# A batched attention and feed-forward kernel: part of q loaded first, four score pairs computed ahead, and bulk loads placed later in the queue

## Chip, cores and metric

One NeuronCore of one Trainium2 chip runs the whole kernel. The metric is the device time of one execution in microseconds (us). Three runs of the kernel before took 929.06, 928.07 and 927.72 us; their median is 928.07 us.

## What is computed

The reference is an attention with two mixings over heads, and a feed-forward layer on its result. Batch 4, 12 heads, 448 positions, head width 64, model width 768, hidden width 2048, all in 32-bit floats.

```python
scores = scale * np.matmul(q, k.transpose(0, 1, 3, 2))
scores = np.einsum('bhij,hg->bgij', scores, w_pre)
scores = scores - np.max(scores, axis=-1, keepdims=True)
attn = np.exp(scores)
attn = attn / (np.sum(attn, axis=-1, keepdims=True) + 1e-09)
attn = np.einsum('bhij,hg->bgij', attn, w_post)
attn_out = np.matmul(attn, v)
x = attn_out.transpose(0, 2, 1, 3).reshape(B * S, H * D)
h = x @ w_in
g = h * (1.0 / (1.0 + np.exp(-1.702 * h)))
return g @ w_out
```

## The kernel before

**Scores.** The queries of a batch are cut into four chunks: three of 120 rows and one of 88 (`chunk`, L204). The 12 heads make six pairs. `scores` (L216) multiplies a chunk of a pair's queries with its keys into two PSUM banks, `keep_scores` (L244) copies both banks to SBUF on ScalarE or VectorE, and `send_scores` (L248) writes the pair to a DRAM scratch `sd` of that chunk. The scratch is there to change the layout: `gather` (L256) reads ten query rows of all 12 heads back as one tile `r` of 120 partitions, which needs all six pairs of the chunk.

**Steps.** Ten query rows are one step: 12 steps to a chunk, 45 to a batch, 180 in all (the last of a batch is smaller). A step mixes heads with one product (`mix`, L266, tile `mx`), takes the row maximum on VectorE (`peak`), the exponential on ScalarE (`expo`), scales the second mixing's weights by the row sums on GpSimd (`shifted`, `weigh_mix`) and multiplies again (`post_whole`, L310, tile `pp`). There are four `r` buffers, so that four steps are gathered ahead. After the 12 steps of a chunk `context` (L383) multiplies with v in two halves (tile `av`, one PSUM bank), and ScalarE and VectorE bring the result into x as a pair of 16-bit parts.

**Weights and feed-forward.** The weights of the feed-forward layer come in 16 pieces (two kinds, eight slices). Each is loaded in three parts of 512 KB (L466), rounded and split on VectorE and ScalarE (tile `w_f`, some 18 VectorE instructions), and stored to DRAM as a 16-bit pair `wd` (L532); the sum of squares of a piece goes through TensorE (`pp<-w_m`, L108). From about step 53 on the feed-forward products of the first batch (`hidden`, tile `h`, L557; `project`, tile `po`, L595) fill TensorE beside the steps of the later batches. After the last step only feed-forward work is left.

**What sets the order.** The program is written out at build time. The head (L775 to L845) is in a fixed order: loads of k and q in thirds, ten products on ones, the six score pairs of the first chunk, each sent for its first 48 rows only (`FRONT`), four gathers, the remaining 72 rows of each pair, and 16 more products on ones (`idle_products`), whose results are not used. Behind it a list scheduler (`add`, `run_all`) holds a model of the engines and of the DMA queue, takes tasks by due step, and so fixes the order on each engine. On the chip every engine runs its own instructions strictly in that order and waits on semaphores. All DMAs are issued by SyncE (SP), one after the other; one issue waits until the eighth issue before it has landed. The scheduler's rule is in `run_all`: a DMA starts at the earliest when the eighth before it is over.

## Time and profile before

| | |
|---|---|
| median of 3 runs | 928.07 us |
| the profiled execution | 930.12 us |
| its span, first to last instruction | 928.4 us |
| PE busy | 897.2 us, 97% of the span |
| VectorE, ScalarE, GpSimd busy | 589.4, 593.3, 337.8 us |
| mean granted TensorE clock | 0.992 |
| moved by DMA | 196.76 MB, mean 212 GB/s |

PE is TensorE; its busy time is modelled for matmuls that overlap, so that a busy PE may still run slowly. A granted clock of 1.00 is the upper of its two levels, 2.4 GHz, and 0.50 the lower; a number between says how a stretch is shared by both. A matmul of 32-bit data has two records. The times of rows count from the first instruction of the span. A window's row gives, behind its length, how long each engine was busy in it.

### The profile page before, as it was taken

The numbers are of one execution on the slowest core, as the hardware profiler recorded it, in microseconds if no ns is written. First come the engines' busy times: TensorE is split into PE (matmuls) and PEld (weight loads), VectorE is DVE, ScalarE is ACT, GpSimd is POOL, SyncE is SP. The second block draws the span as 40 slices with busy tenths as digits, with TensorE's granted clock in tenths as the row PEclk, the third lists the DMA queues.
The fourth block names the chain that finished last, engine by engine and source line by source line (L and its number), as shares of the span: only waits on it lengthen the run. The fifth ranks groups of instructions, "written<-read, shape, count | busy, mean of one in ns | idle before, by whom it ended". The sixth has DMA issues, their size and how long they took to land.

```text
span 928.4 us, 18998 instructions
## 1 busy us (share of the span) xinstructions
PE 897.2 (97%) x6972; PEld 535.5 (58%) x6972; DVE 589.4 (63%) x1342; ACT 593.3 (64%) x1328; POOL 337.8 (36%) x532
## 2 busy tenths in 40 slices
PE   7879989999999999989999999999999999999998
PEld 5455656656566566655656555555656666545554
DVE  2678787687789978977567656567555554332233
ACT  2668787697875776765696776666675665324342
POOL 0212222221225313546346744455344553203431
PEclk9999999999999999999999999999999999999999
DMA  7878999997988796669576575567443422343322
GB/s 235 288 257 298 321 305 329 320 314 230 335 294 287 231 299 207 204 194 328 168 249 221 162 238 162 164 176 255 140 154 111 129 99 83 123 133 132 136 75 88
DMA packets 66256, 196.76 MB, mean 212 GB/s; under 512 B 7699, under 2 KB 32403, under 8 KB 66163
## 3 DMA queue, kind: packets, MB, share of 16 engines
q1 hardware_dynamic: 66162, 195.54, 65.1%
q8 instruction: 55, 0.90, 0.4%
q14 instruction: 39, 0.31, 0.1%
HBM read 138.89 MB, written 56.62 MB: 211 GB/s over the span
## 4 chain that ended last, share of the span: by engine, by line
PE 75%; DVE 9%; DMA 6%; ACT 5%; issue 2%; POOL 2%; SPq 1%; ACTq 0%; POOLq 0%; DVEq 0%
PE po L595 20%; PE h L557 20%; PE mx L271 12%; PE pp L316 5%; PE av L394 3%; PE av L405 3%; PE qk L225 3%; PE qk L235 3%; DMA r<-sd 2%; PE pp L353 2%; PE pp L355 2%; PE pp L354 2%; DVE nm L278 2%; ACT e L285 1%; ACT waste L96 1%
## 5 line engine op out<-in xcount | busy, mean ns | idle before, releaser
L557 PE MATMUL h<-x,wt 128*128 128x448 f16 x1152 | 246.8, 352 | 3.2 <-DMA wt<-wd 2.9
L595 PE MATMUL po<-g,wt 128*128 128x448 f16 x1152 | 239.7, 352 | 4.3 <-DVE th L576 2.4
L271 PE MATMUL mx<-r,wa 120*120 120x448 f32 x360 | 172.3, 563 | 5.2 <-DMA r<-sd 3.1
L557 PEld LDWEIGHTS <-wt 128*128 128x128 f16 x1152 | 109.2, 98 | 115.5 <-issue 26.4
L285 ACT ACTIVATE e<-mx,nm 120x448 f32<-120x448 f32 x180 | 113.9, 633 | 96.4 <-DVE nm L278 84.5
L595 PEld LDWEIGHTS <-wt 128*128 128x128 f16 x1152 | 109.9, 98 | 108.4 <-issue 16.7
L296 POOL TENSOR_SCALAR rs<-sm 120x1 f32<-120x1 f32 x180 | 46.8, 260 | 336.6 <-ACT e L285 333.3
L278 DVE TENSOR_REDUCE nm<-mx 120x1 f32<-120x448 f32 x180 | 111.4, 619 | 46.3 <-PE mx L271 44.9
L623 POOL TENSOR_TENSOR acc<-acc,pt 128x448 f32<-128x448 f32 x64 | 72.8, 1138 | 117.3 <-ACT pt L617 116.9
L316 PEld LDWEIGHTS pp<-wr,e 120*112 120x112 f32 x720 | 84.4, 177 | 40.9 <-issue 18.9
L576 DVE SCALAR_TENSOR_TENSOR th<-th,h 128x448 f32<-128x448 f32 x64 | 39.6, 619 | 105.9 <-ACT th L572 105.5
L340 POOL TENSOR_TENSOR a<-w,a 120x448 f16<-120x448 f32 (+1 forms) x90 | 95.8, 1064 | 26.3 <-POOL w L326 17.6
L316 PE MATMUL pp<-wr,e 120*112 120x120 f32 x720 | 91.4, 270 | 6.0 <-POOL wr L306 6.0
L246 ACT COPY sc<-qk 120x448 f32<-120x448 f32 (+1 forms) x150 | 74.5, 532 | 15.7 <-PE qk L225 11.3
L619 DVE SCALAR_TENSOR_TENSOR acc<-po,ct,acc 128x448 f32<-128x448 f32 x104 | 70.3, 679 | 22.0 <-PE po L595 21.1
L271 PEld LDWEIGHTS mx<-r,wa 120*120 120x120 f32 x360 | 57.8, 184 | 37.4 <-issue 16.2
L326 POOL TENSOR_SCALAR w<-e,rs 120x448 f32<-120x448 f32 (+1 forms) x90 | 60.5, 672 | 40.8 <-DVE rs L301 35.0
L617 ACT ACTIVATE pt<-po,ct 128x448 f32<-128x448 f32 x64 | 40.6, 634 | 51.1 <-PE po L595 51.0
L334 ACT ACTIVATE a<-e,rs 120x448 f16<-120x448 f32 (+1 forms) x90 | 60.3, 670 | 18.4 <-DVE rs L301 17.2
L380 DVE TENSOR_TENSOR p<-pp,p 112x480 f16<-112x480 f32 (+1 forms) x90 | 58.4, 649 | 19.2 <-ACT p L376 18.9
L306 POOL TENSOR_SCALAR wr<-wp,rs 120x120 f32<-120x120 f32 (+1 forms) x90 | 47.4, 527 | 54.0 <-DVE rs L301 33.7
L353 PE MATMUL pp<-wp,a 120*112 120x120 f16 x360 | 62.3, 217 | 0.0
(123 smaller groups left out, 1323.0 us busy)
## 6 DMA issues: line engine op xcount, KB each, us to landing
wt<-wd SPq DMA_DIRECT2D x64, 768.0 KB
r<-sd SPq DMA_DIRECT2D x176, 210.0 KB
sd<-sc SPq DMA_DIRECT2D x66, 420.0 KB
w<-in_moe_w_in_dram SPq DMA_DIRECT2D x24, 512.0 KB
w<-in_moe_w_out_dram SPq DMA_DIRECT2D x24, 512.0 KB
wd<-w_p SPq DMA_DIRECT2D x16, 768.0 KB
sd<-sc SPq DMA_DIRECT2D x24, 308.0 KB
out_dram<-acc SPq DMA_DIRECT2D x24, 224.0 KB
```

Of the source, the lines that this page charges most:

```text
L246: (nc.scalar.copy if eng == "A" else nc.vector.tensor_copy)(t[:n, x, :], two[x][:n, :S])
L271: nc.tensor.matmul(mx[:K, :S], st["wa", b][:K, :K], row.pop(("r", i))[:K, :], start=True, stop=True)
L278: nc.vector.tensor_reduce(nm[:K], row["mx", i][:K, :S], axis=AX.X, op=ALU.max, negate=True)
L285: nc.scalar.activation(e[:K], row.pop(("mx", i))[:K, :S], AF.Exp, bias=row.pop(("nm", i))[:K, 0:1], scale=1.0, accum_out=sm[:K, 0:1],)
L316: nc.tensor.matmul(pp[:CP, jc * K:(jc + 1) * K], e[:K, jc * CP:(jc + 1) * CP], wr[:K, :, :n], start=True, stop=True,)
L326: nc.gpsimd.tensor_scalar(w[:K], e[:K], row["rs", i][:K, 0:1], 1.0, op0=ALU.mult, op1=ALU.mult)
L340: nc.gpsimd.tensor_tensor(a2[:K], row.pop(("w", i))[:K], row["a1", i][:K], op=ALU.subtract)
L353: nc.tensor.matmul(o, a1[:K, js], wp1[:K, :, :n], start=True, stop=False)
L557: nc.tensor.matmul(h, w[:, i, c, fc * 128:(fc + 1) * 128], x[:, j, c, :], start=(n == 0), stop=(n == len(terms) - 1),)
L595: nc.tensor.matmul(po, w[:, j, fc, e * 128:(e + 1) * 128], g[:, i, fc, :], start=(n == 0), stop=(n == len(terms) - 1),)
L619: nc.vector.scalar_tensor_tensor(a, po, c, a, op0=ALU.mult, op1=ALU.add)
L623: nc.gpsimd.tensor_tensor(a, a, st.pop(("pt", u, e)), op=ALU.add)
```

## The change

Three things are changed. The first third-by-third loads of q bring only the first 240 of 448 columns (two chunks of queries); the other 208 columns come by three loads of their own, behind the back sends of the first chunk. Four of the six score pairs of the second chunk (`SOON`) are computed, copied and sent in the head, between the first chunk's pairs and the first step, and idle products fall from 16 to 4. And the scheduler gets a kind of load, "late" (the weight parts, their stores, v, and q and k of later batches): it holds such a DMA in its model until its queue has at most 1.5 us of work left. The due time of a score send falls from x + 2 to x.

```diff
--- before.py
+++ after.py
@@ -121,6 +121,17 @@
         t = st[name, b, i] = flow.tile(SH[name], F32, name=f"{name}{use}{i}_{b}", tag=tag, bufs=THIRDS)
         w = t.shape[1]
         nc.sync.dma_start(out=t, in_=SRC[name][b][:, i * w:(i + 1) * w])
+
+    def load_front(i, n):
+
+        t = st["q", 0, i] = flow.tile(SH["q"], F32, name=f"qf{i}_0", tag=f"qp{i}")
+        w = t.shape[1]
+        nc.sync.dma_start(out=t[:, :, :n], in_=q[0][:, i * w:(i + 1) * w, :n])
+
+    def load_back(i, n):
+        t = st["q", 0, i]
+        w = t.shape[1]
+        nc.sync.dma_start(out=t[:, :, n:], in_=q[0][:, i * w:(i + 1) * w, n:])
 
     def load_whole(name, b, i):
 
@@ -718,6 +729,8 @@
                     s = max(room, j["from"], free.get(e, 0.0))
                     if j["size"] and len(lanes) >= 8:
                         s = max(s, lanes[-8])
+                    if j["kind"] == "late":
+                        s = max(s, DMA["free"] - 1.5)
                     best.append((s + (j["bias"] if e != j["eng"][0] else 0.0), s, j))
                 if best:
                     t = min(x[0] for x in best) + LOOK
@@ -773,8 +786,8 @@
         return k
 
     for i in range(THIRDS):
-        for name in "kq":
-            load_whole(name, 0, i)
+        load_whole("k", 0, i)
+        load_front(i, 2 * CI)
     for i, w in enumerate((w_pre, w_post)):
         nc.sync.dma_start(out=wrep[:, i, :], in_=w.unsqueeze(0).to_broadcast([GI, H, H]))
     nc.sync.dma_start(out=wall, in_=w_post.unsqueeze(0).to_broadcast([128, H, H]))
@@ -823,12 +836,16 @@
     tags = [("gen", 3), ("mx", 2), ("pp", 2)]
     homes = [("sc", 3), ("g", 2), ("sc", 3), ("g", 2), ("sc", 3), ("acc", 1)]
     kept = []
-    FRONT = 48
+    FRONT, SOON = 48, 4
+
+    def head_pair(c, pr, tag, home):
+        two = scores(0, c, pr, tag)
+        kept.append(scores_home(0, c, pr, home))
+        for x in range(2):
+            keep_scores(0, c, x, kept[-1], two, "AD"[x])
+
     for pr in range(NPAIR):
-        two = scores(0, 0, pr, tags[pr % 3])
-        kept.append(scores_home(0, 0, pr, homes[pr]))
-        for x in range(2):
-            keep_scores(0, 0, x, kept[pr], two, "AD"[x])
+        head_pair(0, pr, tags[pr % 3], homes[pr])
         send_scores(0, 0, pr, kept[pr], 0, FRONT)
     nc.vector.tensor_tensor(
         w_mix,
@@ -837,16 +854,22 @@
         op=ALU.mult,
     )
     mixing(0)
+    for pr in range(SOON):
+        head_pair(1, pr, tags[pr % 3], (f"wt{pr % 2}", 2))
     mixing_pair()
     for i in range(AHEAD):
         gather(i)
     for pr in range(NPAIR):
         send_scores(0, 0, pr, kept[pr], FRONT)
-    idle_products(16)
-
-
-    free.update({"PE": 17.0, "A": 15.0, "D": 16.0, "G": 3.0, "SP": 21.0})
-    DMA["free"] = 22.0
+    for i in range(THIRDS):
+        load_back(i, 2 * CI)
+    for pr in range(SOON):
+        send_scores(0, 1, pr, kept[NPAIR + pr])
+    idle_products(4)
+
+
+    free.update({"PE": 17.5, "A": 16.0, "D": 18.0, "G": 3.0, "SP": 22.0})
+    DMA["free"] = 26.0
     lanes.extend([24.0] * 8)
     held["sc"] = [23.0, 23.5, 24.0]
     r_home = {i: [] for i in range(N)}
@@ -932,7 +955,7 @@
                     {"A": 0.53, "D": 0.62}, bias=0.3)
             banks[n].append(k)
             both.append(k)
-        s = add("SP", 0.4, lambda: send_scores(b, c, pr, t["t"]), both, x + 2, size=0.43)
+        s = add("SP", 0.4, lambda: send_scores(b, c, pr, t["t"]), both, x, size=0.43)
         sc += both + [s]
         sends.setdefault((b, c), []).append(s)
 
@@ -975,11 +998,11 @@
 
     def whole_load(name, b, i, x):
         h = in_home[name, b, i]
-        return add("SP", 0.4, lambda: load_whole(name, b, i), gated_by(x), x, size=0.459, takes=[(f"{name}p{i}", h)])
+        return add("SP", 0.4, lambda: load_whole(name, b, i), gated_by(x), x, size=0.459, takes=[(f"{name}p{i}", h)], kind="late")
 
     def staged_load(name, b, i, use, x):
         h = []
-        return add("SP", 0.4, lambda: load(name, b, i, use), gated_by(x), x, size=0.459, takes=[("op", h)]), h
+        return add("SP", 0.4, lambda: load(name, b, i, use), gated_by(x), x, size=0.459, takes=[("op", h)], kind="late"), h
 
     def split_tasks(name, b, x):
         for i in range(THIRDS):
@@ -998,7 +1021,7 @@
         for a in range(NP):
             w64, wf = [], []
             wfs.append(wf)
-            j = add("SP", 0.4, lambda a=a: c["fetch"](a), gated_by(first + 2 * a), first + 2 * a, size=0.524, takes=[("w64", w64)])
+            j = add("SP", 0.4, lambda a=a: c["fetch"](a), gated_by(first + 2 * a), first + 2 * a, size=0.524, takes=[("w64", w64)], kind="late")
             for n, (name, occ) in enumerate((("magnitude", 0.36), ("least", 0.35), ("shift", 0.35), ("rest", 0.61), ("sign", 0.61))):
                 j = add("D", occ, lambda a=a, name=name: c[name](a), [j], due, occ + 0.09, takes=[] if n else [("wf", wf)])
                 w64.append(j)
@@ -1016,7 +1039,7 @@
             low.append(add("D", 0.66, lambda a=a: c["w_lower"](a), [u], due + 0.5, 0.75))
             wfs[a] += [u, low[a]]
             pair += [low[a]] + ([u] if a else [])
-        j = conv_done[kind, s] = add("SP", 0.4, c["store"], low, due, size=0.786)
+        j = conv_done[kind, s] = add("SP", 0.4, c["store"], low, due, size=0.786, kind="late")
         pair.append(j)
 
 
@@ -1029,7 +1052,9 @@
             for pr in range(NPAIR):
                 x = base - (18 if c == NCH - 1 else 17) + 2 * pr if c else base - 11 + pr
                 if b == 0 and c == 1:
-                    x = pr
+                    if pr < SOON:
+                        continue
+                    x = pr - SOON
                 at_scores.setdefault(max(x, 0), []).append((b, c, pr))
     at = {}
     for b in range(B):
```

What the scheduler makes of it differs by hundreds of rows. Three places are shown. In the names, `qk_c_p_x` is chunk c, pair p and head x of the pair; `mx` and `pp` are the two products of a step, `r` its gathered rows, `sums` the idle products.

TensorE from the last score pair of the first chunk to the second step, before:

```order
L225 MATMUL qk_0_5_0_194<-kf_0_130,qf_0_132 120x448
L225 MATMUL qk_0_5_1_195<-kf_0_130,qf_0_132 120x448
L786 MATMUL sums<-ones 128x128 x16
L271 MATMUL mx_245<-r_215,wa_203 120x448
L225 MATMUL qk_1_0_0_247<-kf_0_122,qf_0_124 120x448
L225 MATMUL qk_1_0_1_248<-kf_0_122,qf_0_124 120x448
L271 MATMUL mx_253<-r_217,wa_203 120x448
```

and with the change:

```order
L236 MATMUL qk_0_5_0_194<-kf_0_130,qf_0_132 120x448
L236 MATMUL qk_0_5_1_195<-kf_0_130,qf_0_132 120x448
L236 MATMUL qk_1_0_0_205<-kf_0_122,qf_0_124 120x448
L236 MATMUL qk_1_0_1_206<-kf_0_122,qf_0_124 120x448
L236 MATMUL qk_1_1_0_212<-kf_0_122,qf_0_124 120x448
L236 MATMUL qk_1_1_1_213<-kf_0_122,qf_0_124 120x448
L236 MATMUL qk_1_2_0_219<-kf_0_126,qf_0_128 120x448
L236 MATMUL qk_1_2_1_220<-kf_0_126,qf_0_128 120x448
L236 MATMUL qk_1_3_0_226<-kf_0_126,qf_0_128 120x448
L236 MATMUL qk_1_3_1_227<-kf_0_126,qf_0_128 120x448
L799 MATMUL sums<-ones 128x128 x4
L282 MATMUL mx_268<-r_243,wa_203 120x448
```

Four pairs of the second chunk stand ahead of the first step, and twelve idle products fewer.

SyncE's queue behind the back sends of the first chunk (72 rows each), before; `w_0_64` is a part of the weights, `vf` one third of v, `r` a gather:

```order
L250 DMA sd_0_90<-sc_0_5_198 72x896
L261 DMA r_311<-sd_0_90 120x448
L466 DMA w_0_64_0_313<-in_moe_w_in_dram 128x1024
L261 DMA r_322<-sd_0_90 120x448
L466 DMA w_0_64_1_329<-in_moe_w_in_dram 128x1024
L250 DMA sd_1_91<-sc_1_0_299 120x896
L261 DMA r_340<-sd_0_90 120x448
L250 DMA sd_1_91<-sc_1_1_326 120x896
L261 DMA r_348<-sd_0_90 120x448
L466 DMA w_0_64_2_353<-in_moe_w_in_dram 128x1024
L129 DMA vf_0_364<-in_v_dram 112x1024
L261 DMA r_374<-sd_0_90 120x448
```

and with the change:

```order
L261 DMA sd_0_90<-sc_0_5_198 72x896
L134 DMA qf_0_124<-in_q_dram 128x2x208
L134 DMA qf_0_128<-in_q_dram 128x2x208
L134 DMA qf_0_132<-in_q_dram 128x2x208
L261 DMA sd_1_91<-sc_1_0_209 120x896
L261 DMA sd_1_91<-sc_1_1_216 120x896
L261 DMA sd_1_91<-sc_1_2_223 120x896
L261 DMA sd_1_91<-sc_1_3_230 120x896
L272 DMA r_327<-sd_0_90 120x448
L261 DMA sd_1_91<-sc_1_4_314 120x896
L272 DMA r_337<-sd_0_90 120x448
L272 DMA r_345<-sd_0_90 120x448
```

The fifth gather (the first `r` here) stood directly behind the back sends; now three loads of q's rest and four sends of the second chunk are ahead of it. The loads of weights and v are behind it by more: the first weight part comes as the sixth row after it.

TensorE around the end of the first chunk's steps, where its context product `av` (two halves, `av_0_0` and `av_0_3`) and the first step of the second chunk stand, before:

```order
L316 MATMUL pp_601<-wr_593,e_572 112x120 x4
L316 MATMUL pp_619<-wr_616,e_598 112x120 x4
L108 MATMUL pp_619<-mv_467,ones 128x6
L394 MATMUL av_0_0_651<-p_0_287,vf_0_364 64x120 x16
L394 MATMUL av_0_0_651<-p_0_287,vf_0_409 64x120 x8
L394 MATMUL av_0_3_695<-p_0_287,vf_0_409 64x120 x8
L394 MATMUL av_0_3_695<-p_0_287,vf_0_496 64x120 x16
L271 MATMUL mx_724<-r_625,wa_203 120x448
```

and with the change, from the thirteenth step's mixing to the first half:

```order
L282 MATMUL mx_562<-r_462,wa_203 120x448
L327 MATMUL pp_569<-wr_546,e_518 112x120 x4
L282 MATMUL mx_587<-r_481,wa_203 120x448
L108 MATMUL pp_569<-w_0_m,ones 128x3
L327 MATMUL pp_599<-wr_583,e_559 112x120 x4
L282 MATMUL mx_622<-r_505,wa_203 120x448
L236 MATMUL qk_2_3_0_631<-kf_0_126,qf_0_128 120x448
L236 MATMUL qk_2_3_1_632<-kf_0_126,qf_0_128 120x448
L327 MATMUL pp_641<-wr_627,e_615 112x120 x4
L282 MATMUL mx_657<-r_541,wa_203 120x448
L405 MATMUL av_0_0_666<-p_0_310,vf_0_500 64x120 x16
L405 MATMUL av_0_0_666<-p_0_310,vf_0_527 64x120 x8
```

Before, both halves stand next to each other ahead of the thirteenth mixing. Now the 13th to the 16th mixing precede the first half, and the second half (not shown) stands four mixings behind it.

## Rows read from the trace of the kernel before

**Rows 1.** The page, parts 1 and 2: engines over the span, granted clock per slice.
```profile
PE 897.2 (97%) x6972; PEld 535.5 (58%) x6972; DVE 589.4 (63%) x1342; ACT 593.3 (64%) x1328; POOL 337.8 (36%) x532
...
PEclk9999999999999999999999999999999999999999
```

**Rows 2.** Windows: stretch, length, busy (records) of PE, PEld, DVE, ACT, POOL; clock, DMA, GB/s.
```profile
0.00:31.00 31.00, 25.39 (x127) 16.38 (x128) 10.53 (x29) 10.99 (x23) 2.94 (x15) 0.94 0.71 225
31.00:75.00 44.00, 36.36 (x237) 22.02 (x236) 33.19 (x86) 30.46 (x77) 8.11 (x22) 0.92 0.81 279
75.00:100.00 25.00, 24.70 (x163) 15.62 (x163) 21.01 (x52) 20.43 (x51) 5.87 (x20) 1.00 0.94 318
100.00:200.00 100.00, 94.77 (x697) 61.16 (x694) 76.30 (x200) 77.21 (x196) 25.54 (x67) 0.98 0.99 318
200.00:290.00 90.00, 90.00 (x633) 56.24 (x632) 75.46 (x189) 67.43 (x162) 22.09 (x42) 1.00 0.86 290
290.00:400.00 110.00, 104.53 (x778) 64.12 (x776) 95.78 (x215) 77.20 (x182) 41.83 (x61) 1.00 0.76 242
400.00:800.00 400.00, 398.82 (x3709) 236.91 (x3707) 237.24 (x493) 266.65 (x573) 197.41 (x278) 1.00 0.56 176
800.00:928.40 128.40, 122.60 (x647) 63.02 (x644) 39.88 (x81) 42.97 (x67) 34.01 (x30) 1.00 0.33 114
```

**Rows 3.** Timeline from 8 to 35 us: start, length, engine, line, operation, [idle before <- releaser].
```profile
8.53 1.77 PE L225 MATMUL qk<-kf,qf 64*120 64x448 f32 x8 [0.82 <-DMA qf<-in_q_dram]
...
10.81 1.77 PE L225 MATMUL qk<-kf,qf 64*120 64x448 f32 x8 [0.51 <-DMA qf<-in_q_dram]
...
12.51 3.84 PE L786 MATMUL sums<-ones 128*128 128x128 f32 x32
...
16.14 1.68 SPq L261 DMA_DIRECT2D r<-sd  x4
...
19.00 0.98 PE L271 MATMUL mx<-r,wa 120*120 120x448 f32 x2 [2.66 <-DMA r<-sd]
...
27.32 1.02 PE L225 MATMUL qk<-kf,qf 64*120 64x448 f32 x4
...
27.63 0.32 SPq L261 DMA_DIRECT2D r<-sd  x1
...
31.13 0.92 PE L271 MATMUL mx<-r,wa 120*120 120x448 f32 x2
```

**Rows 4.** DMA issues by line, with the size of one.
```profile
r<-sd SPq DMA_DIRECT2D x176, 210.0 KB
sd<-sc SPq DMA_DIRECT2D x66, 420.0 KB
...
kf<-in_k_dram SPq DMA_DIRECT2D x6, 448.0 KB
```

**Rows 5.** Windows of three stretches at a lower clock.
```profile
20.00:25.00 5.00, 4.50 (x10) 1.63 (x11) 1.94 (x4) 1.51 (x5) 0.56 (x2) 0.67 0.77 276
35.00:40.00 5.00, 4.39 (x14) 1.65 (x15) 4.12 (x9) 3.50 (x9) 0.94 (x4) 0.70 1.02 349
65.00:70.00 5.00, 5.00 (x40) 3.73 (x36) 1.67 (x4) 1.93 (x6) 0.00 (x0) 0.73 0.01 4
```

**Rows 6.** Timeline of PE from 54 to 72 us.
```profile
58.52 2.68 PE L394 MATMUL av<-p,vf 112*64 112x120 f32 x48 [0.66 <-ACT p L372]
63.74 4.34 PE L394 MATMUL av<-p,vf 112*64 112x120 f32 x48 [2.54 <-DVE x L428]
68.02 1.01 PE L271 MATMUL mx<-r,wa 120*120 120x448 f32 x2
```

**Rows 7.** Windows with much VectorE work; the last is of tile w_f alone (DVE, ACT).
```profile
150.00:250.00 100.00, 97.37 (x676) 61.31 (x673) 76.74 (x201) 77.16 (x189) 21.47 (x54) 0.98 0.94 303
290.00:320.00 30.00, 27.82 (x161) 16.45 (x159) 28.00 (x62) 19.64 (x46) 12.99 (x17) 1.00 0.76 245
...
150.00:250.00 100.00, 42.56 (x78) 17.76 (x38) 0.98 0.94 303
```

## The prediction

> **What bounds the kernel now.** I read the page's totals first, then the span cut into stretches, then the timeline of the head, then the places where the clock falls. The totals [rows 1] say that TensorE is busy 97% of the span. The stretches [rows 2] say where the missing 31.2 us lie: 5.6 us idle up to 31 us, 7.6 from 31 to 75, 0.3 from 75 to 100, 5.2 from 100 to 200, none from 200 to 290, 5.5 from 290 to 400, 1.2 from 400 to 800 and 5.8 in the tail. The clock adds a loss that busy time hides: 0.94 over the first 31 us and 0.92 over the next 44. A mean of 0.92 over 44 us means that 16% of it, 7.0 us, ran at half speed, and half of that, 3.5 us, is lost. From 400 us on TensorE simply works; what is there to win lies ahead of 200 us, above all from 31 to 75 us with 7.6 + 3.5 = 11.1 us lost.
>
> The second resource to watch is the DMA queue: 0.94 to 0.99 busy from 75 to 200 us at 318 GB/s, but 0.71 and 0.81 ahead of that [rows 2]. From 65 to 70 us it is at 0.01 [rows 5]. That is one hole, and the timeline shows it [rows 6]: the two halves of the first context product stand next to each other on TensorE, the second waits 2.54 us for VectorE to free the one PSUM bank, runs at the low clock for 4.34 us where the first took 2.68, and the thirteenth step's mixing, which is queued behind it, starts at 68.02 us. Meanwhile no step runs, no row buffer comes free, no gather can be issued.
>
> **The pace behind.** By the order, both programs have the same feed-forward and attention products ahead of each mixing from about the 69th step on, to the end. So I take the stretch behind that as unchanged, and the question is how much earlier the program gets there. The sum stands against the profiled execution, 930.12 us, and its differences are carried to the median of the runs, 928.07 us.
>
> **Term 1: the head up to the fifth mixing, +2.3 us.** A third of k and q (896 KB) takes 2.28 us, from 8.53 to 10.81 us [rows 3]. Three loads of q lose 208 KB each, 624 KB in all: 1.6 us less before the last score pairs, so the front sends, the gathers now issued at 16.14 us and the first mixing at 19.00 us [rows 3] come 1.6 us sooner. No row shows packets of 960 bytes; if the shorter rows cost as much as the whole ones, this gain is 0. The Trainium skill, "DMA: Bandwidth & Descriptors", Specifications, has transfers keep their rate from 512 bytes on, which would leave 1.6; no run here shows it yet.
>
> The first four pairs of the second chunk then run in the wait for the gathers. One pair is 1.02 us [rows 3], four are 4.1; they take the place of twelve of the 16 idle products (3.84 us for 16, 0.24 each [rows 3]), which had only filled the wait. They cost nothing on the path: the last pair of the first chunk would end at 12.5 - 1.6 = 10.9 us, the four at 15.0, four idle products at 16.0, the first gather lands at 17.4. Their copies fall on VectorE and ScalarE, which are busy 10.5 and 11.0 of the first 31 us [rows 2] and wait with TensorE here.
>
> But the fifth gather now waits longer. Before, it is issued at 27.63 us, when the back sends have landed, and its mixing starts at 31.13 [rows 3]. Now the back sends have landed at 26.0, and ahead of it in the same queue are 624 KB of q and four sends of 420 KB [rows 4], 2304 KB. At 349 GB/s [rows 5] that is 6.8 us, and 0.6 for its own 210 KB: 33.4 us, so +2.3. Bounds: 29.5 if all of it moves beside the back sends, whose stretch from 20 to 25 us shows a share of 0.77 only [rows 5]; 36.9 if the rate is 318 GB/s and the whole 3.5 us from issue to mixing come on top. I take 33.4, since the stretch from 30 us on ran at 349 with much the same mix of transfers.
>
> **Term 2: work done ahead, -3.1 us.** By the order twelve score pairs precede the fifth mixing, against nine before. Three pairs fewer remain, 3 x 1.02 [rows 3].
>
> **Term 3: the loss from 31 to 75 us, -7.9 us.** It was 11.1. Four of the second chunk's six sends stand ahead of the fifth gather, the loads of weights and v behind it, and the two context halves are four mixings apart, so that the bank is freed while steps run. What remains: a wait of about 5 us ahead of the fifth mixing (in term 1) is followed by a stretch at the low clock, as the waits of 2.66 and 2.54 us were [rows 3, 5, 6]: five microseconds at 0.67 are 1.7 lost. The fifth to eighth steps still come at the pace of their gathers, with a send of 420 KB in between: about 1.0. The rest at the pace of 75 to 100 us, 0.3 per 25 [rows 2]: 0.5. Together 3.2, so 11.1 - 3.2 = 7.9 are won. Bounds: 3 if another hole of the old kind (2.5 idle, 1.7 at the low clock) stays in it, 11 if none does.
>
> A rule stands against this part of the change: the Trainium skill, "TensorE: Matmul & The Clock Gate", Why this matters for your kernels, advises against idle gaps between bursts of matmuls, since the clock then falls; dropping twelve filler products while the wait grows does the opposite. The trace agrees where a gap is long [rows 5, 6]; without such a fall the sum would be 1.7 us better.
>
> **Term 4: weights later, +2.0 us.** Loads marked late move the early weight pieces back. By the order six pieces have their sum between the 44th and 69th mixing, five before. One piece is 42.56 us x 18 / 78 = 9.8 us of VectorE [rows 7], and VectorE has 23 of 100 us free from 150 to 250 [rows 7]. With it VectorE would be 87% busy. At 77% TensorE is idle 2.6% of the time, at 93% (290 to 320 us) 7.3% [rows 7]; half-way is 5%, some 2 us more over the stretch. Bounds: 9.8 if nothing of it is hidden; -4 if the shorter queue also gives back most of the 5.2 us idle from 100 to 200 us [rows 2]. SyncE issues the same transfers plus three; the order by the gather of step 64 has 59.9 MB ahead of it, 62.7 before, so the queue is not asked for more.
>
> **Sum.** 2.3 - 3.1 - 7.9 + 2.0 = -6.7 us: 930.12 becomes 923.4, and the median 928.07 becomes **921.4 us**. The terms' bounds together move this by some 6 us either way.
>
> **Rivals.** *More is won.* The fifth mixing comes at 31 us or before and no new hole opens: term 1 gives 0 or less, term 3 the full 10, term 4 nothing: about -13, 915 us. For it speaks the DMA share of 0.77 in the head; against it that every stretch ahead of 200 us has its own waits.
>
> *Given back: no change.* What "late" does is in the scheduler's model alone; on the chip SyncE tests no queue length, it only meets the loads at other places. If its model puts the transfers of the head too early, the fifth mixing comes at 36.9 us (+5.8), and the bunched weights cost 5: 5.8 - 3.1 - 7.9 + 5 = -0.2, 927.9 us. For it speaks that VectorE is above 90% busy from 290 us on [rows 7].
>
> *Slower: the DMA queue runs dry.* Loads that stood ahead of gathers kept the queue full. Now they stand behind gathers that wait for a row buffer, thus for a step; each such wait stops SyncE, and the queue empties behind it. From 75 to 290 us the rows give 25 x 318 + 100 x 318 + 90 x 290 = 65.9 MB at a mean of 306 GB/s [rows 2]. At 290 GB/s the same bytes take 227 us, 12 more; -6.7 + 12 = +5.3, 933.4 us. It decides from 297 GB/s on, where the loss equals the gain, if the gathers are what TensorE waits for. Against it speak the fewer bytes ahead of step 64 and that TensorE is never idle from 200 to 290 us at a DMA share of 0.86 [rows 2]; for it the share of 0.99 ahead of that, where nothing is spare.
>
> **How the numbers follow.** The forecast's case (917 to 926 us) gets 0.52, more won 0.16, given back 0.13, slower 0.19. A measurement tells 0.2%, about 1.9 us, from no change: faster is below 926.2, 0.52 + 0.16 = 0.68; the same up to 929.9, 0.13; slower 0.19. The range from 914.5 to 930.5 us leaves out some 0.05 of the better case and 0.15 of the slower one.
>
> **What would show it.** In the changed profile: first mixing near 17.4 us; fifth near 33.4, with a low clock behind its wait; thirteenth mixing well under 60 us instead of at 68.02; no stretch of 5 us with a DMA share near 0; idle plus clock loss from the fifth mixing to 75 us near 3 us; idle time behind 290 us as before. I am wrong in kind if the thirteenth mixing comes early and the end does not move (then terms 3 and 4 cancel later), or if the DMA rate from 75 to 290 us falls under 297 GB/s while TensorE waits for gathers.

## The result: 0.85% slower

Timed side by side, the changed kernel takes 938.07 us (median of six runs, 934.12 to 938.83), the kernel before 929.32 (927.72 to 930.67): a ratio of 1.0085, 95% interval 1.0063 to 1.0107. The forecast was 921.4 us, faster. The profiled execution of the changed kernel, 934.12 us, is the fastest of its six, so its trace shows only half of the loss: its span grew by 3.9 us. What is read from traces below is of these two executions (930.12 and 934.12 us).

The page after, engines and granted clock per slice (answers to [rows 1]):

```profile
PE 896.9 (96%) x6948; PEld 530.9 (57%) x6948; DVE 599.1 (64%) x1354; ACT 586.1 (63%) x1314; POOL 347.8 (37%) x537
...
PEclk8899998999999999999999999999999999999999
```

The windows of after, columns as in [rows 2]:

```profile
0.00:31.00 31.00, 25.26 (x115) 14.74 (x116) 12.61 (x33) 12.05 (x25) 2.94 (x15) 0.89 0.77 227
31.00:75.00 44.00, 34.80 (x206) 20.68 (x204) 27.47 (x73) 28.82 (x75) 9.56 (x27) 0.92 0.99 294
75.00:100.00 25.00, 22.55 (x160) 14.52 (x159) 21.18 (x58) 20.33 (x52) 6.61 (x18) 1.00 0.89 282
100.00:200.00 100.00, 96.92 (x729) 63.61 (x728) 73.21 (x191) 71.48 (x179) 22.86 (x63) 0.97 0.95 306
200.00:290.00 90.00, 88.33 (x620) 54.30 (x618) 74.93 (x193) 71.25 (x173) 24.22 (x44) 1.00 0.89 288
290.00:400.00 110.00, 103.62 (x760) 62.92 (x757) 101.41 (x216) 75.01 (x176) 46.75 (x60) 0.98 0.78 247
400.00:800.00 400.00, 398.77 (x3638) 234.40 (x3639) 246.02 (x509) 261.77 (x565) 200.55 (x281) 1.00 0.58 179
```

TensorE's idle time grew from 31.2 to 932.3 - 896.9 = 35.4 us, by 4.2, which covers the whole growth of the span. Against [rows 2] the stretches differ by +0.1 (head), +1.6 (31 to 75 us), +2.2, -2.2, +1.7, +0.9 and about 0. Busy time stayed the same although twelve idle products (2.9 us) are gone: the rest of the work took longer, at a mean granted clock of 0.985 after 0.992. These are stretches of equal time, not of equal work; the mixings, further down, are the better marks.

The stretch that the forecast was about, cut once more, after:

```profile
31.00:60.00 29.00, 21.00 (x102) 12.16 (x100) 15.30 (x40) 16.32 (x43) 5.43 (x16) 0.88 0.98 291
60.00:75.00 15.00, 13.80 (x104) 8.52 (x104) 12.17 (x33) 12.50 (x33) 4.14 (x11) 1.00 1.01 300
75.00:290.00 215.00, 207.80 (x1506) 132.43 (x1505) 169.32 (x440) 163.06 (x402) 53.69 (x125) 0.98 0.92 296
```

and before:

```profile
31.00:60.00 29.00, 24.62 (x139) 13.49 (x139) 22.07 (x58) 21.80 (x56) 6.28 (x16) 0.94 1.00 346
60.00:75.00 15.00, 11.73 (x102) 8.54 (x99) 11.13 (x29) 8.66 (x21) 1.83 (x6) 0.89 0.45 149
75.00:290.00 215.00, 209.47 (x1485) 133.02 (x1484) 172.77 (x440) 165.08 (x407) 53.50 (x128) 0.99 0.93 307
```

The hole of [rows 5, 6] is closed: from 60 to 75 us the queue moves 300 GB/s instead of 149. But the stretch ahead lost as much: with the queue as full as before (0.98 against 1.00), it moved 291 GB/s where it had moved 346, and TensorE worked 21.0 us of 29 where it had worked 24.6.

The timeline of TensorE in the head and at three later places, after:

```profile
14.53 1.16 PE L799 MATMUL sums<-ones 128*128 128x128 f32 x8
18.66 1.82 PE L282 MATMUL mx<-r,wa 120*120 120x448 f32 x2 [2.97 <-DMA r<-sd]
...
35.67 1.85 PE L282 MATMUL mx<-r,wa 120*120 120x448 f32 x2 [4.34 <-DMA r<-sd]
38.82 1.85 PE L282 MATMUL mx<-r,wa 120*120 120x448 f32 x2 [1.31 <-DMA r<-sd]
...
54.00 0.92 PE L282 MATMUL mx<-r,wa 120*120 120x448 f32 x2
...
60.42 1.01 PE L282 MATMUL mx<-r,wa 120*120 120x448 f32 x2 [1.78 <-ACT e L296]
...
93.89 1.07 PE L327 MATMUL pp<-wr,e 120*112 120x120 f32 x8 [2.44 <-POOL wr L317]
...
154.09 1.47 PE L282 MATMUL mx<-r,wa 120*120 120x448 f32 x2 [1.73 <-DMA r<-sd]
```

SyncE's queue in the head, after:

```profile
15.80 1.68 SPq L272 DMA_DIRECT2D r<-sd  x4
17.52 6.45 SPq L261 DMA_DIRECT2D sd<-sc  x6
24.01 2.35 SPq L134 DMA_DIRECT2D qf<-in_q_dram  x3
26.47 4.25 SPq L261 DMA_DIRECT2D sd<-sc  x4
30.81 1.13 SPq L272 DMA_DIRECT2D r<-sd  x1
```

The first mixing comes at 18.66 us (19.00 before), the fifth at 35.67 (31.13 [rows 3]), the thirteenth at 54.00 (68.02 [rows 6]). The third last row shows a new wait. TensorE lacks the exponential of the thirteenth step. Its maximum is found at 55.6, but ScalarE starts it only at 59.66, since sums over two thirds of v stand ahead of it, and the second of these loads, issued at 50.30, is there at 58.28. ScalarE from 55 to 60 us, after:

```profile
55.52 0.63 ACT L96 ACTIVATE waste<-vf 112x512 bf16<-112x512 f32 x1 [0.49 <-DMA vf<-in_v_dram]
...
58.28 0.63 ACT L96 ACTIVATE waste<-vf 112x512 bf16<-112x512 f32 x1 [0.83 <-DMA vf<-in_v_dram]
...
59.66 0.61 ACT L296 ACTIVATE e<-mx,nm 120x448 f32<-120x448 f32 x1
```

What SyncE waits for longest from 75 to 290 us, before and after (engine, line, what it waited for: us, times, longest):

```profile
SPq L261 <- PE mx L271: 56.8, 39, 6.7
```

```profile
SPq L272 <- PE mx L282: 69.4, 46, 5.5
```

Gathers wait 12.6 us longer for a row buffer, and nothing else is issued meanwhile. But TensorE hardly waits for gathers there. What it waits for in the same stretch, after:

```profile
PE pp L327 <- POOL wr L317: 4.8, 3, 2.4
PE mx L282 <- DMA r<-sd: 1.7, 1, 1.7
```

**At equal work.** Every step has one mixing, so the n-th mixing marks the same point of both programs. Against the kernel before, the fifth comes 4.5 us later, the thirteenth 14.0 sooner, the 50th 8.8 sooner (166.56 after 175.31), the 69th 0.3 sooner (244.90 after 245.20), the 100th 5.2 later (411.80 after 406.60) and the 180th, the last, 4.2 later. At the 69th mixing the lead is gone, and the whole loss of this execution lies behind it, where TensorE has the same number of records (x5445). From the 69th mixing to the end, before and after:

```profile
245.20:928.40 683.20, 670.75 (x5445) 392.05 (x5443) 412.29 (x886) 418.77 (x898) 286.36 (x389) 1.00 0.57 183
```

```profile
244.90:932.30 687.40, 674.13 (x5445) 391.23 (x5443) 424.01 (x896) 415.63 (x894) 296.44 (x394) 1.00 0.58 184
```

The loss is between the 80th and the 100th mixing. That stretch, and in the second row its work on the weights alone (tile `w_f`, VectorE and ScalarE), before:

```profile
300.79:406.60 105.81, 101.42 (x771) 62.11 (x770) 87.56 (x204) 73.96 (x173) 38.16 (x57) 1.00 0.71 224
300.79:406.60 105.81, 43.18 (x69) 16.78 (x36) 1.00 0.71 224
```

and after:

```profile
299.02:411.80 112.78, 105.51 (x772) 63.32 (x771) 99.48 (x223) 77.46 (x181) 46.75 (x63) 0.97 0.74 233
299.02:411.80 112.78, 52.27 (x84) 18.95 (x42) 0.97 0.74 233
```

It is 7.0 us longer: TensorE is idle 2.9 us more, and the granted clock is 0.97 instead of 1.00. VectorE has 9.1 us more of weight work in it, and from the 69th to the 80th mixing 8.2 us less (15.22 after 23.40): weight work has moved back past the 80th mixing. That it is this work which lengthens the stretch is argued, not shown, since no run moves it alone.

### The profile page after: what moved, and what is told of

It reads as the page before. It is cut to its first block, busy times and chain, and to the rows that moved or that the text cites. A ratio compares the mean times of both kernels' runs of the same rounds, so it can differ in the third digit from the quotient of the medians.

```text
span 932.3 us, 18977 instructions
## 1 busy us (share of the span) xinstructions
PE 896.9 (96%) x6948; PEld 530.9 (57%) x6948; DVE 599.1 (64%) x1354; ACT 586.1 (63%) x1314; POOL 347.8 (37%) x537
## 4 chain that ended last, share of the span: by engine, by line
PE 79%; DVE 10%; DMA 5%; ACT 3%; issue 1%; POOL 1%; SPq 0%; ACTq 0%; POOLq 0%
PE h L568 22%; PE po L606 20%; PE mx L282 13%; PE pp L327 6%; PE qk L236 4%; PE av L416 3%; PE qk L246 3%; PE av L405 3%; PE pp L364 2%; PE pp L366 2%; PE pp L365 2%; DVE w_p L537 1%; DVE nm L289 1%; DVE w_f L498 1%; ACT e L296 1%
## 5 line engine op out<-in xcount | busy, mean ns | idle before, releaser
L282 PE MATMUL mx<-r,wa 120*120 120x448 f32 x360 | 177.8, 578 | 15.4 <-DMA r<-sd 10.3
L606 PEld LDWEIGHTS <-wt 128*128 128x128 f16 x1152 | 110.7, 98 | 113.8 <-issue 21.8
L634 POOL TENSOR_TENSOR acc<-acc,pt 128x448 f32<-128x448 f32 x67 | 76.9, 1148 | 118.4 <-ACT pt L628 118.2
L630 DVE SCALAR_TENSOR_TENSOR acc<-po,ct,acc 128x448 f32<-128x448 f32 x101 | 68.4, 679 | 19.5 <-PE po L606 19.2
L257 ACT COPY sc<-qk 120x448 f32<-120x448 f32 (+1 forms) x136 | 68.0, 532 | 13.6 <-PE qk L236 9.4
L628 ACT ACTIVATE pt<-po,ct 128x448 f32<-128x448 f32 x67 | 42.5, 634 | 51.6 <-PE po L606 51.4
L387 ACT CAST p<-pp 112x480 f16<-112x480 f32 (+1 forms) x90 | 50.2, 558 | 21.3 <-PE pp L366 21.1
```

Source lines behind the costliest of these rows:

```text
L257: (nc.scalar.copy if eng == "A" else nc.vector.tensor_copy)(t[:n, x, :], two[x][:n, :S])
L282: nc.tensor.matmul(mx[:K, :S], st["wa", b][:K, :K], row.pop(("r", i))[:K, :], start=True, stop=True)
L606: nc.tensor.matmul(po, w[:, j, fc, e * 128:(e + 1) * 128], g[:, i, fc, :], start=(n == 0), stop=(n == len(terms) - 1),)
L630: nc.vector.scalar_tensor_tensor(a, po, c, a, op0=ALU.mult, op1=ALU.add)
L634: nc.gpsimd.tensor_tensor(a, a, st.pop(("pt", u, e)), op=ALU.add)
```

## The experiments

In the kernels called "order held", and in x6, x5 and x10, the scheduler's own run is replaced by a list of its tasks (`PLAN`, packed), taken from the kernel before or from a changed one:

```diff
-    run_all()
...
+    for key, e in json.loads(zlib.decompress(base64.b85decode(PLAN))):
...
+        j = every[key]
...
+        j["f"](e) if len(j["eng"]) > 1 else j["f"]()
```

A key names a task by the call that makes it and a count: 4 is a mixing, 21 the send of a pair, 40 a gather. Times are medians beside the kernel before in the same comparison; the ratio is taken over all runs, so it need not be the quotient of the medians; "rate" is GB/s from 75 to 290 us in the profiled execution (before 307); "late" says by how many us this execution is behind the traced one of the kernel before at the fifth mixing, at the 69th and at the end of the span. The change itself has +4.5, -0.3, +3.9.

| kernel | us | before | ratio, 95% interval | rate | late |
|---|---|---|---|---|---|
| x1 head, old order held | 934.99 | 930.40 | 1.0045 (1.0021 to 1.0070) | 308 | +4.7, +1.8, +1.4 |
| x6 as x1, old queue places | 930.52 | 929.80 | 1.0011 (0.9990 to 1.0031) | 304 | -0.1, +3.1, +1.6 |
| x5 sends behind gathers | 940.43 | 930.40 | 1.0109 (1.0091 to 1.0126) | 289 | -0.8, +6.6, +10.4 |
| x10 filler in the waits | 937.70 | 930.67 | 1.0076 (1.0050 to 1.0102) | 296 | +4.4, +0.3, +5.5 |
| e2 head, replanned | 936.08 | 930.40 | 1.0064 (1.0046 to 1.0082) | 291 | +4.9, +5.6, +5.4 |
| e1 late alone, 1.5 us | 936.65 | 930.40 | 1.0074 (1.0047 to 1.0100) | 291 | -0.1, +1.4, +5.3 |
| e1c late alone, 3.0 us | 934.83 | 930.67 | 1.0033 (1.0003 to 1.0063) | 300 | +0.8, +0.5, +6.6 |
| e1b late alone, 5.0 us | 925.20 | 929.80 | 0.9956 (0.9934 to 0.9979) | 307 | +0.1, -2.9, -1.0 |
| e4 whole change, 5.0 us | 928.77 | 930.67 | 0.9983 (0.9958 to 1.0009) | 301 | +5.7, +0.2, +0.4 |
| n1 model latency 2.3 | 934.27 | 929.80 | 1.0044 (1.0019 to 1.0070) | 303 | -0.1, +1.4, +3.5 |
| n2 model rate 0.305 | 942.41 | 929.80 | 1.0130 (1.0100 to 1.0161) | 292 | +1.5, +6.9, +12.9 |
| n3 model latency 2.1 | 929.72 | 930.67 | 0.9983 (0.9965 to 1.0000) | 306 | +0.8, +0.8, -0.2 |
| x12 loads late, old order held | 1079.97 | 930.62 | 1.1611 (1.1577 to 1.1646) | 180 | -0.3, +117.0, +147.2 |
| x13 loads early, e1's order held | 949.50 | 930.62 | 1.0214 (1.0190 to 1.0238) | 285 | +0.3, +15.5, +19.3 |
| x14 loads early, after's order held | 943.82 | 930.62 | 1.0139 (1.0119 to 1.0160) | 288 | +4.3, +8.0, +12.8 |

**The head: x1, x6, x5, x10, e2.** x1 has the head of the change and, behind it, every engine's old order. x6 differs from x1 in one thing: q's rest and the four sends stand where these sends stood before.

```diff
-    for i in range(THIRDS):
-        load_back(i, 2 * CI)
-    for pr in range(SOON):
-        send_scores(0, 1, pr, kept[NPAIR + pr])
...
+        if key in ("21#1", "21#2", "21#3", "21#4"):
+            pr = int(key[-1]) - 1
+            send_scores(0, 1, pr, kept[NPAIR + pr])
+            if pr < THIRDS:
+                load_back(pr, 2 * CI)
```

> The changed head (front of q, four pairs ahead, four idle products) with every later task in the order of the kernel before, written out as a list; no late loads. Theory A (the head's seven transfers ahead of the fifth gather delay it, the wait costs idle time and a slow clock, and the later order only passes it on): the fifth mixing stays near 35.7 us, the hole around the first context products stays too, since that order has both halves together; the time is 3 to 8 us over the kernel before. Theory B (the loss comes from the new order behind the head: late loads stand behind gathers that wait): the head is harmless, three pairs of 1.02 us are saved, and the time is within 2 us of the kernel before or up to 4 us under it.

> The changed head's products (front of q, four pairs ahead, four idle products) with the order of the kernel before behind it, and with the four sends of the second chunk at the places in SyncE's queue that they had before, one of the three loads of q's rest behind each of the first three. Theory A (from 20 to 60 us the DMA queue is the bound; transfers put ahead of the fifth gather cost what they take): the fifth mixing is back near 31 us, the loss of 4.6 us of the run with the old order goes, and the time is within 2 us of the kernel before or up to 3 us under it. Theory C (it is the score pairs run ahead, or the split of q, that cost, wherever the sends stand): the time stays 3 to 6 us over the kernel before.

The fifth mixing of x1, then that of x6, in TensorE's timeline:

```profile
35.83 1.85 PE L282 MATMUL mx<-r,wa 120*120 120x448 f32 x2 [7.96 <-DMA r<-sd]
```

```profile
31.00 1.85 PE L282 MATMUL mx<-r,wa 120*120 120x448 f32 x2 [2.20 <-DMA r<-sd]
```

x1 is 4.6 us slower than before, and its fifth mixing is as late as that of the change; x6 takes the time of before, and its fifth mixing comes as before. That the seven transfers ahead of the fifth gather delay the fifth mixing, by 4.8 us, is shown. What that costs at the end is less sure. By the ratios x1 and x6 are 0.34% apart, some 3 us, and with both intervals anything from 0 to 6. In the two traced executions (931.50 us, one of x1's fastest, and 931.68) nothing is left of it: x1 regains 2.9 us by the 69th mixing, x6 loses 3.3, and its ninth mixing already comes at 46.25 us after 43.78 before. Four pairs computed ahead with a smaller first load of q win nothing clear of noise even where the fifth gather is not delayed (-0.9 to +2.9 us).

x5 keeps the change's own order and only moves the seven transfers behind the eighth gather:

```diff
+        if key == "40#4":
+            for n in range(THIRDS):
+                load_back(n, 2 * CI)
+            for pr in range(SOON):
+                send_scores(0, 1, pr, kept[NPAIR + pr])
```

> The changed kernel in its own order, written out as a list, but with the three loads of q's rest and the four sends of the second chunk moved behind the eighth gather. Theory A: the fifth mixing starts near 29 to 31 us instead of 35.7, the wait of 4.3 us ahead of it and one slow-clock stretch go, and 4 to 7 us of the changed kernel's 938 are won back. Theory B: the head's gain is passed on to the next wait for the queue; the time moves by less than 2 us from 938.

The fifth and the ninth mixing of x5:

```profile
32.15 1.86 PE L282 MATMUL mx<-r,wa 120*120 120x448 f32 x4 [0.93 <-DMA r<-sd]
...
46.16 1.82 PE L282 MATMUL mx<-r,wa 120*120 120x448 f32 x2 [8.42 <-DMA r<-sd]
```

The wait left the fifth mixing and came back, longer, at the ninth. In one block the transfers hold up whichever gather is behind them. Theory A fell: nothing of the 938 us is won back; the time is by the ratios some 2 us more, with intervals that overlap.

x10 is the changed kernel with 16 idle products ahead of the first and 16 ahead of the fifth mixing.

```diff
-    idle_products(4)
+    idle_products(16)
...
+        if key == "4#5":
+            idle_products(16)
```

> The changed kernel in its own order, written out as a list, with idle products put into its two long waits: 16 instead of 4 ahead of the first mixing, and 16 ahead of the fifth (3.84 us of products each). Nothing else moves. Theory K (the low clock behind these waits costs time): the two stretches at the low clock behind them, 6.8 us each, go or shrink, and 2 to 5 us of the changed kernel's 938 are won back. Theory A (the DMA queue is the bound there): the clock is kept but the gathers land when they did; less than 1.5 us is won.

From 18 to 25 us the clock of x10 is 1.00, where the change ran at 0.54 from 17.5 to 25:

```profile
18.00:25.00 7.00, 6.58 (x30) 3.36 (x32) 3.46 (x8) 3.21 (x9) 1.67 (x6) 1.00 0.78 255
```

But the fifth mixing still starts at 35.53 us, and the time does not move. The fall of the clock behind the first wait is free: without it TensorE only gets sooner to its wait for the same gather. The 16 products ahead of the fifth mixing did not do what they were put in for: 3.63 us of waiting are left behind them, and the clock is at 0.56 from 35 to 42 us (0.51 in the change):

```profile
35.00:42.00 7.00, 5.83 (x12) 2.61 (x13) 2.11 (x5) 1.54 (x5) 0.75 (x3) 0.56 0.91 290
```

Whether the fall behind the fifth mixing's wait costs anything x10 therefore doesn't tell.

e2 is the change without the late kind and with sends due at x + 2, replanned.

```diff
-                    if j["kind"] == "late":
-                        s = max(s, DMA["free"] - 1.5)
...
+        s = add("SP", 0.4, lambda: send_scores(b, c, pr, t["t"]), both, x + 2, size=0.43)
```

> Only the head (front of q, four pairs ahead, four idle products, the scheduler's start times for it), planned anew without late loads and with sends due two steps after their scores. Theory A: the fifth mixing is as late as in the changed kernel, near 35.7 us, and the time is 4 to 9 us over the kernel before. Theory B: without late loads the time is at the kernel before or up to 6 us under it.

Its fifth mixing comes at 36.07 after a wait of 5.90 us, and it is about as slow as x1.

**The late kind: e1, e1c, e1b, e4.** e1 is the kernel before with the kind alone; e1c and e1b let the model's queue hold 3.0 and 5.0 us, e4 is the whole change with 5.0.

```diff
+                    if j["kind"] == "late":
+                        s = max(s, DMA["free"] - 5.0)
```

> Only the late kind of loads, with the head and the due times of the kernel before, planned anew. Theory A: no transfers ahead of the fifth gather, so it comes near 31 us as before; the hole from 58 to 70 us shrinks since loads no longer stand ahead of the second chunk's sends; the time is 2 to 8 us under the kernel before. Theory B: the loads behind waiting gathers leave the queue short of work, the rate from 75 to 290 us falls from 306 to under 297 GB/s, and the time is 4 to 10 us over the kernel before.

> Late loads only, held until the model's queue has 3.0 us of work left: between the runs with 1.5 (6 us over the kernel before) and 5.0 (4 us under it). Theory B (a shorter queue costs in proportion): 0 to 4 us over the kernel before, DMA rate from 75 to 200 us between 300 and 313 GB/s. Theory N (each plan is a draw): anywhere from 4 us under to 13 us over, with no relation to the threshold.

> Late loads only, as in the run before, but held only until the model's queue has 5.0 us of work left instead of 1.5. Theory B (short queue costs in proportion): the order differs far less from the kernel before, the rate from 75 to 200 us is back near 318 GB/s, and the time is within 2 us of the kernel before. Theory N (any new plan of this scheduler costs some 5 us against the present one): 4 to 7 us over the kernel before.

> The whole change, but with late loads held only until the model's queue has 5.0 us of work left. Theory A with B: the head still costs its 4 us and the late loads no longer do: 2 to 5 us over the kernel before, the fifth mixing near 35 us. Theory N: anywhere from 4 us under to 13 us over.

e1, windows and two gaps of TensorE:

```profile
31.00:60.00 29.00, 26.20 (x144) 14.95 (x145) 20.00 (x49) 22.35 (x56) 7.28 (x21) 1.00 0.97 318
60.00:75.00 15.00, 14.44 (x144) 10.65 (x140) 12.18 (x35) 11.01 (x30) 3.68 (x11) 1.00 0.99 311
75.00:290.00 215.00, 203.19 (x1429) 129.25 (x1429) 167.27 (x434) 160.66 (x394) 48.11 (x118) 0.97 0.89 291
```

```profile
90.78 1.54 PE L316 MATMUL pp<-wr,e 120*112 120x120 f32 x6 [4.30 <-POOL wr L306]
...
184.85 1.85 PE L271 MATMUL mx<-r,wa 120*120 120x448 f32 x2 [5.23 <-ACT e L285]
```

This is the forecast's third term by itself: from 31 to 75 us TensorE is idle 3.4 us at the full clock, where it had been idle 7.6 at 0.92, and the thirteenth mixing comes 15.0 us sooner. At the 69th nothing is left of it. Behind 75 us the rate falls to 291 GB/s and the time is 0.7% longer, but this is not the rival "slower": from 75 to 290 us TensorE never waits for a gather. Its two long waits, of 4.3 and 5.2 us, are for GpSimd and ScalarE, and behind both stands VectorE with weights. From 85.61 to 89.69 us VectorE has nothing but `w_f` tiles, and the reciprocal of 0.15 us that GpSimd needs comes only then; the maximum that ScalarE needs for the second starts at 183.32, without a pause of VectorE before it.

The longer the queue that the model allows, the better in these three plans: +0.74%, +0.33%, -0.44%. e1b beats both kernels, which neither of its texts expected; its 307 GB/s are of its slowest execution, 929.13 us. e4, expected 2 to 5 us over by its first theory, is level with the kernel before, although its fifth mixing is 5.7 us late:

```profile
36.84 1.85 PE L282 MATMUL mx<-r,wa 120*120 120x448 f32 x2 [4.83 <-DMA r<-sd]
```

So the delay in the head need not come out at the end. The stretch from the 80th to the 100th mixing takes 111.0 us in e1, 114.6 in e1c, 108.3 in e1b, 108.2 in e4 and 108.1 in e2, where there are no late loads; VectorE's work on `w_f` in it is 51.2, 46.6, 45.3, 45.5 and 44.6 us. The most weight work there goes with the threshold of 1.5, but e1c shows that the stretch can be long without it.

**The draw of a plan: n1, n2, n3.** The kernel before, with one number of the scheduler's model changed a little:

```diff
-    DMA = {"free": 0.0, "rate": 0.31, "late": 2.2, "issue": 0.4}
+    DMA = {"free": 0.0, "rate": 0.305, "late": 2.2, "issue": 0.4}
```

> The kernel before with one number of the scheduler's model changed that has to do with nothing here: the landing time of a DMA 2.3 instead of 2.2 us. Theory N: the plan changes in many places and the time is 3 to 8 us over the kernel before, as with every plan made anew. Theory B: it is within 3 us of the kernel before, and the DMA rate from 75 to 200 us stays at 310 GB/s or more.

> The same with the model's DMA rate at 0.305 instead of 0.31. Theory N: 3 to 8 us over the kernel before. Theory B: within 3 us of it.

> The kernel before with the model's landing time of a DMA at 2.1 instead of 2.2 us; the plan differs in far fewer places than with 2.3. Theory N: a third draw, between 4 us under and 13 us over the kernel before; the mean of the three draws stays over it by 3 us or more, since the present plan is one of the better ones.

Nothing is meant to be better or worse in them, and they differ by -0.17% to +1.30%. One new plan is as fast as that of before, two are slower, and n2 is slower than either of its texts has it; three are too few to say where the plan of before stands among all. The 0.74% of e1 can't be read as the price of its rule alone, nor the 0.44% of e1b as its gain, and the 0.85% of the whole change lies in the same spread.

**The places of the loads alone: x12, x13, x14.** TensorE, VectorE, ScalarE and GpSimd keep their order instruction for instruction; only SyncE's list changes. The diff is in the list: each late load stands as many gathers later (x12) or earlier (x13, x14) as the texts say.

> The kernel before with the order of every engine held, but SyncE's list changed: the loads of weights, of v and of later q and k (and the stores of the lower weights) stand where the planner of the late kind (threshold 1.5 us) puts them, counted in gathers, as far as their first user in the list lets them: 71 of 112 stand behind 1 to 10 gathers more than before. Theory L (a load late in the queue is the cost of the late kind): 934 to 938 us (ratio 1.005 to 1.009), the rate in 100-200 us falls from 318 to about 305 GB/s and a wait of an earlier engine on a load appears there. Theory R (the redrawn order of the other engines is the cost, the late places alone are harmless): 928 to 931 us, ratio within 0.002 of 1.

> The kernel with the late kind alone (936.65 us), every engine's order held but SyncE's: the late loads go forward to the places that they have before, counted in gathers, as far as the buffers that they fill allow: 61 of 112 go forward, by 1 to 9 gathers; 77 then stand exactly where they stand before. Theory L: 926 to 931 us (the cost goes with the places; the order behind the closed hole at 58-70 us then shows its gain). Theory R: 935 to 938 us, as with the late places.

> The whole change (938.1 us) with its order held on every engine but SyncE, where the late loads go forward by 1 to 9 gathers (64 of 112) to about the places of before. Theory L: 930 to 934 us: the cost of the late places (about 6) goes, that of the head (about 4) stays and is partly offset by the closed hole. Theory R: 936 to 939 us.

Both theories fell. What VectorE waits for in x12 from 31 to 290 us:

```profile
DVE w_f L473 <- DMA w<-in_moe_w_in_dram: 57.2, 10, 11.2
DVE w_f L473 <- DMA w<-in_moe_w_out_dram: 34.3, 8, 7.3
```

and SyncE in x13 from 75 to 290 us:

```profile
SPq L261 <- PE mx L271: 43.5, 31, 4.9
...
SPq L466 <- DVE w_f L493: 11.1, 8, 2.4
...
SPq L466 <- DVE w_f L477: 5.9, 4, 1.9
```

In x12 the loads come later and their users don't, so VectorE stands still in front of them, 91.5 us in all, and the maxima of the steps behind it. The price of a late load in an order that doesn't expect it is thus far above the 6 us at issue. In x13 the gathers wait less for row buffers (43.5 us, in e1 64.1), as intended, but SyncE now waits 17 us for weight buffers that VectorE has not freed, with the gathers behind, and the time rises. x14 is the same on the whole change. The places and the order of the other engines are one choice; these runs give no share of the 0.74% that belongs to the places alone.

## Why the prediction was wrong

**The sum at its own point.** The prediction put all its gain ahead of the 69th mixing, 6.7 us. There the change leads by 0.3. Up to the fifth mixing it lost 4.5 us instead of 2.3, and from there to the 69th it won 4.8 where terms 2 to 4 together have 9.0. And the step "So I take the stretch behind that as unchanged" failed: TensorE has the same products there, but they took 4.2 us more: 7.0 more between the 80th and the 100th mixing, less elsewhere. Equal work on TensorE was no equal pace here; VectorE's work beside it had moved. All this is of one execution of each kernel; where the other 5 us or so of the medians' 8.75 lie, no trace shows.

**Term 1 had the right mechanism and too small a size.** +2.3 us was forecast to the fifth mixing; it came 4.5 us later (35.67 after 31.13). Two steps failed. The gain of 1.6 us ahead of the first gathers was 0.34: the last front send is issued 1.0 us sooner (12.32 after 13.31 us), but its last packet is over 3.00 us after its issue instead of 2.35 (packets of 3584 bytes took 297 ns after 274 from 12 to 15 us, where both programs have only sends), and the gathers came at 15.80 after 16.14. And "I take 33.4, since the stretch from 30 us on ran at 349 with much the same mix of transfers" took the row of 35 to 40 us (from 30 to 35 it was 323), a rate from loads, sends and gathers together, and put it on sends and short rows: from 25 to 35 us the change moves 297 GB/s at a share of 0.94, from 35 to 60 us 285.

**Term 2 is worth nothing that can be seen.** "Three pairs fewer remain, 3 x 1.02": the work is gone from the later stretch, but x6, which has four pairs done in the head and its fifth mixing on time, takes the time of before. Up to 60 us the queue is full (a DMA share of 1.00 from 31 to 60 us). In x6 the work taken from TensorE there did not even come back as waiting: from 31 to 60 us TensorE is idle 3.8 us (before 4.4) but runs at a clock of 0.79 (before 0.94), with the DMA share at 1.00. x10 shows another side: a faster clock behind the first wait buys nothing. The claim that the loss of TensorE is what there is to win, from [rows 1, 2], is what these two runs speak against: idle or slow TensorE beside a full DMA queue is a sign of the queue, not a stock of time.

**Term 3 closed the hole and did not keep the gain.** The thirteenth mixing came at 54.00 us, "well under 60" as forecast, and no stretch has an idle queue. But the loss from 31 to 75 us did not fall from 11.1 to 3.2; idle time rose to 9.2 at the same mean clock. I had costed what remains as if the stretch ran on at its rate of before; from 35 to 60 us twelve gathers are issued instead of eight, and it moved 285 GB/s instead of 352. In e1, where the head is the old one, the term came true up to 75 us (3.4 us idle, no fall of the clock), and still e1 is 1.4 us behind at the 69th mixing: what is won at one point is not yet won at a later one. The sign that was named for being wrong in kind, a thirteenth mixing that comes early and an end that does not move, is what came.

**Term 4, and which rival came.** "Loads marked late" were costed as VectorE work ahead of the 69th mixing, +2.0. The work went further back: 9.1 us more of it stand between the 80th and the 100th mixing, where VectorE is busy 88% of the time (before 83%). That is the second half of the rival "given back", the bunched weights at 5 us, as the late fifth mixing is its first half (5.8 there, 4.5 measured); what that rival had wrong was to keep the gains of terms 2 and 3. The rival "slower" has the nearest number, 933.4 us, but by luck. Its sign came, 296 GB/s under 297; its condition, that the gathers are what TensorE waits for, did not: 1.7 us from 75 to 290, and none in e1. Nor did its 12 us: at the 75th mixing the change is 0.8 us ahead (275.40 after 276.16), with 79.60 MB moved instead of 81.80. The lower rate up to there is of fewer bytes asked for, not of time lost. Also not foreseen was the exponential that waited 4 us on ScalarE behind a late third of v.

**The clock.** A fall behind the fifth mixing's wait was forecast and came; at 35 to 42 us the granted clock is 0.51. The Trainium skill, "TensorE: Matmul & The Clock Gate", Why this matters for your kernels, advises against idle gaps between bursts. The trace agrees that the long gaps are followed by the lower clock; in x10 filling the first of them won no time.

**What would have been right.** The head's delay, weight work that moves on behind the 69th mixing, and a fresh plan's draw (-1.6 to +12.1 us) against a hole whose closing is not kept: a forecast of no gain with a wide range to the slow side. Nor did the "some 6 us either way" follow from the terms: their bounds added as squares give about 8 down and 10 up.

**Open.** How much of the loss is the late kind's threshold and how much the new draw. The dose speaks for the threshold, the spread of n1 to n3 is as large as the dose's. And what makes the stretch from the 80th to the 100th mixing long: the weight work on VectorE is there, but e1c and n2 (110.3 us with 45.7 us of it) are long with little more of it than before (43.2).

## What to carry to other kernels

Before idle time of the busiest engine is booked as gain, look at the DMA share of the same stretch: beside a full queue, less work for TensorE (x6) and a faster clock (x10) bought nothing here, and a block of transfers moved ahead came back as a wait at the next gather. Compare two traces at the same step of the work, not at the same time, and follow a gain to the end before it is counted: here 14 us at the thirteenth mixing were 0.3 at the 69th. A planner's plan is one draw: perturb an inert number a few times and take the spread as the noise against which an edit of the planner is judged. Move a load and its user together, or leave both.

## What was not expected of the hardware

**A full queue is not a rate.** From 35 to 60 us the DMA engines are busy nearly all the time in both kernels (a share of 1.00 and 0.98) and move 352 and 285 GB/s. The DMA view of that stretch, before:

```profile
DMA packets 2992, 8.79 MB, mean 352 GB/s; under 512 B 339, under 2 KB 1180, under 8 KB 2988
```

and after:

```profile
DMA packets 2931, 7.12 MB, mean 285 GB/s; under 512 B 325, under 2 KB 1749, under 8 KB 2928
```

The number of packets is the same to about 2%, they are smaller: twelve gathers (rows of 1792 bytes) after eight, four score sends after seven, four loads of weights after three, three of v after two, and no store of weights after one. Each size was slower, too: 101 ns after 81 at 1792 bytes, 167 after 147 at 3584, 242 after 206 at 4096. Why, no run here shows.

**Short rows lose a little.** The front columns of q came in packets of 960 bytes at 51 ns each, 18.7 bytes per ns; the packets of 3584 bytes in the same first 10 us (rows of k, and the first sends) took 164 ns, 21.8 bytes per ns. The Trainium skill, "DMA: Bandwidth & Descriptors", Specifications, has line rate from 512 bytes on; here 960 bytes run at 86% of the longer rows' rate.

**The clock after equal waits.** Each program waits once near 400 us for feed-forward weights, 2.88 us before and 2.64 after. The shorter wait was followed by the lower clock, 0.57 from 400 to 404 us in the change, the longer one in the kernel before was not (1.00 from 394 to 402 us).
